# mLSTM cell and tanh-shrink MLP in fp32: scores on quarter tiles of the array that leave out the quarter under the diagonal

## The chip, the cores and the metric

The kernel runs on one core of one Trainium2 chip. The metric is the device time of one launch in microseconds (us); lower is better.

## What is computed

An mLSTM cell runs over 768 tokens for 4 batches and 8 heads of width 40, and its gated output feeds a small MLP with the activation h - tanh(h). Everything is fp32.

```
for t in range(S):                       # q, k, v: (4, 8, 768, 40)
    m_new = max(f[t] + m, i[t]);  fs = exp(f[t] + m - m_new);  is = exp(i[t] - m_new);  m = m_new
    C = fs * C + is * outer(v[t], k[t]);  n = fs * n + is * k[t]
    y[t] = sigmoid(o[t]) * (C @ q[t]) / max(abs(n . q[t]), 1)
x = y as (3072, 320);  h = x @ w_in (320, 2048);  out = (h - tanh(h)) @ w_out (2048, 320)
```

The kernel computes the recurrence in chunks: within a chunk of 128 tokens, token t needs the products q[t].k[s] for all s <= t (a square of scores of which only the part on and over the diagonal counts, when keys stand in rows and queries in columns), and for all earlier tokens the state at the chunk's start.

## The kernel before

**Units.** A unit is one chunk of 128 tokens of one batch: 6 chunks x 4 batches, 24 units, numbered so that unit n is chunk n // 4 of batch n % 4. Two units make a group of 256 tokens for the MLP; there are 12 groups. The MLP has 2048 hidden features, taken 256 at a time: 8 pairs for each group, two pairs to an item, four items to a group.

**Two stages.** The first 12 units (PLANNED, L1182) and the first 17 items are put in order by a planner with costs for each engine (Plan, L157, run at L1490). From item START (L1186) on, the order is written out by the loop at L1514. Each item of that loop has a dense list of matrix steps: the up products of this item (up, L1023, 16 instructions of 128 columns of weights and 256 tokens, then a remainder on 64 rows, since 320 = 128 + 128 + 64), then cell work, then the down products of the item before (down_seven, L911). The other 12 units each take a slot of two items: in the first, scores(n) follow the remainder (L1523); in the second, block_turned(n) does (L1525). merge (L1146) lays the steps of cell_slot (L853: scaling v, gates, stores) between. An engine carries out its instructions in the order in which this program issues them (Pinned, L96, and T, L116): nothing overtakes within an engine or a queue.

**A later unit's path.** load_unit (L342) issues kz, qz (features first, heads 0 to 3 in rows 0 to 39, heads 4 to 7 in rows 64 to 103), v, k and o on SP's queue, one slot ahead. scaled (L614) multiplies v by a number per token and head, out of ei. scores (L629) makes for each head a square of 128 keys by 128 queries, K = 40, in two banks of PSUM; the two row halves of the array work at once, each with the whole width of weights. mask (L639) multiplies by the matrix upto (ones where key <= query) on DVE and writes P. block_turned (L764) adds up the state's part (old state by qz) and the products of scaled v with P, with 64 x 64 tiles: the 128 keys are the two row halves r, two heads sit in the two column halves c. Row half r writes bank turned[r], so that the two banks have to be summed: turn_back (L807) copies one bank on ACT, adds on DVE, transposes in blocks of 32 on DVE and brings the result to token order by way of DRAM (h_rows, z_in) on SP's queue. gate_turned (L827) divides and gates, and turn_by_store (L735) brings y into xT, features first, again by way of DRAM (y_rows) on SP's queue. update_halves and keep_halves (L789, L800) make the next state out of k and the scaled v.

**Names.** upto (L381) is the 128 x 128 mask. ei (L423) holds the scales by token in rows and by chunk and head in columns; t["wide"] is the scaled v of a unit; HALF is 64, HH is 4, D is 40, D1 is 41 (the extra column gives the denominator). In up, quarters=True takes the remainder with 64 x 64 tiles (quarter, L1040) and False with 64 x 128 tiles (product, L1028); it is True in the items where block_turned follows. in_halves (L752) copies the states of the planned units to the layout of the later ones. PE has one line for all of its products (L129), and all other engines share L106.

Of the kernel before, what the change touches and what calls it, by code (L numbers as in the profile page):

```python
# [60 lines left out]
L = 128  # L61
# [18 lines left out]
def kernel(  # L80
# [258 lines left out]

    ld = {}  # L340

    def load_unit(n, names=("kz", "qz", "v", "k", "o", "q2"), queue=SP, behind=()):  # L342
        c, b = divmod(n, B)
        t = ld.setdefault(n, {})
        for name in names:
            if name in ("kz", "qz"):
                t[name] = load.tile([128, HH, L], FP, name=name, tag=name, bufs=3)
                for i in range(2):
                    src = kT if name == "kz" else qT
                    dma = queue.dma_start(out=t[name][i * HALF:i * HALF + D], in_=src[b, c, :, i * HH:(i + 1) * HH])  # L350
                    if behind:
                        tc.add_manual_dep(dma.ins, behind[-1].ins.name, SYNC, reason="order of transfers")
            elif name == "k":
                if n + B < NU:
                    t["k"] = load.tile([L, WIDE, D], FP, name="k", tag="k", bufs=3)
                    queue.dma_start(out=t["k"].rearrange("p h d -> p (h d)"),
                                    in_=bass.AP(k.tensor, k[b, c].offset, [[H * D, L], [1, WIDE * D]]))
            elif name != "q2":
                src, bufs = {"v": (v, 3), "o": (o_gate, 4)}[name]
                t[name] = load.tile([L, H, D], FP, name=name, tag=name, bufs=bufs)  # L360
                queue.dma_start(out=t[name], in_=src[b, c])
            elif c:
                t["q2"] = load.tile([TOP, len(TRIOS), L], FP, name="q2", tag="q2", bufs=3)
                for i in range(TRIO):
                    queue.dma_start(out=t["q2"][i * D:(i + 1) * D, 0:len(range(i, H, TRIO))], in_=qT[b, c, :, slice(i, H, TRIO)])
# [59 lines left out]


    eN = const.tile([TOP, NU, HH], FP, name="eN")

    begun = []

# [183 lines left out]
    def scaled(n, i, name, bufs, by_heads=False):  # L614
# [2 lines left out]
        flat = att.tile([L, H * D1 + HALF - D1], FP, name=name, tag=name, bufs=bufs)  # L617
        to = flat[:, 0:H * D1].rearrange("p (h d) -> p h d", d=D1)
        t["wide"] = flat
        scale = ei[:, i, t["c"], t["hs"]]  # L620
        t["column"] = lambda: A.copy(out=to[:, :, D], in_=scale)
        if by_heads:
            for h in range(H):
# [5 lines left out]
    def scores(n):  # L629
# [5 lines left out]
        def product(j, i):  # L635
            rows = slice(i * HALF, i * HALF + D)
            T.matmul(ps[i][:, j, :], t["kz"][rows, j, :], t["qz"][rows, j, :], start=True, stop=True)
# [12 lines left out]

        masks = [(lambda i=i: copy(i), lambda i=i: select(i)) if n in BY_POOL and not t.get("decays") else lambda i=i: mask(i) for i in range(2)]
        return [lambda j=j, i=i: product(j, i) for j in range(HH) for i in range(2)], masks

    def halves(*parts):

        for first in (0, 1):
            for steps in parts:
                for step in steps[first]:
                    step()
# [104 lines left out]
    def block_turned(n):  # L764
# [12 lines left out]
                    T.matmul(t["turned"][i][c * HALF:(c + 1) * HALF, i * 2 + g, :], old[rows, j * D1:j * D1 + HALF], t["qz"][rows, j, :],  # L777
                             start=(g == 0), stop=False, skip_group_check=True)
        for i in range(2):
            for g in range(2):  # L780
                for c in range(2):
                    for r in range(2):
                        rows, j = slice(r * HALF, (r + 1) * HALF), 2 * g + c
                        at = (i * HH + j) * D1
                        T.matmul(t["turned"][r][c * HALF:(c + 1) * HALF, i * 2 + g, :], t["wide"][rows, at:at + HALF], t["P"][rows, i, j, :],
                                 start=False, stop=True, skip_group_check=True)
        update_halves(n)

    def update_halves(n):  # L789
# [17 lines left out]
    def turn_back(n):  # L807
# [3 lines left out]
        both = att.tile([128, 2, HH * L // BLOCK, BLOCK], FP, name="zt", tag="P", bufs=4)  # L811
        zt, added = both[:, 0], both[:, 1].rearrange("p b i -> p (b i)")
        flat = zt.rearrange("p b i -> p (b i)")
        A.copy(out=added, in_=t["turned"][1].rearrange("p g t -> p (g t)"))
        V.tensor_tensor(out=added, in0=t["turned"][0].rearrange("p g t -> p (g t)"), in1=added, op=OP.add)
        V.transpose(flat, added)
        rows = dram.tile([2, 2, HH, L, BLOCK], FP, name="h_rows", tag=f"h_rows{n % 4}")
        for a in range(128 // BLOCK):
            half, low = divmod(a, 2)
# [33 lines left out]
    def cell_slot(s, o):  # L853
# [2 lines left out]
        steps, pause = [], [(0.0, lambda: None)]  # L856
        if s is not None:
            if s + 1 < NU and s + 1 not in ld:
                load_unit(s + 1, ("kz", "qz", "v", "k", "o"))
            begin(s)  # L860
        if o is None:
            return [(0.0, lambda: prepare(s))]
# [644 lines left out]
    for p in range(SPLIT):  # L1507
        spread_over([(0.0, lambda p=p: [step() for _, step in sums_of_weights(p)])], START + p / 2, START + 0.5 + p / 2)
    banks[:] = [name for name in ("b0", "b1") if name != third["tag"]]
    load_unit(PLANNED, ("kz", "qz", "v", "k", "o"))  # L1510
    for b in range(B):
        in_halves(b)
    news = []
    for x in range(START, len(items) + LAG):  # L1514
# [4 lines left out]
                new.append(slot[0])  # L1519
        if x < len(items):  # L1520
            some = tuple(run[:2] for run in items[x])
            dense, rest = up(some, shrink(x), bool(scored))
            dense.append((0.6 + 0.9 * len(new[:1]), lambda: halves(rest, *(scores(n) for n in new[:1]))))  # L1523
            for n in scored:
                dense.append((1.9, lambda n=n: [block_turned(n), Clock.later("turned", 1.2, lambda: [turn_back(n), n + B < NU and keep_halves(n)])]))  # L1525
        dense += [(0.9, lambda n=n: halves(scores(n))) for n in new[1 if x < len(items) else 0:]]
        some = tuple(run[:2] for run in items[x - LAG])
        if in_seven(*some[0]):
            dense += down_seven(some)
# [207 lines left out]
```

## Time and profile before

| | |
|---|---|
| runs, median of 3 | 520.84 us (517.76 to 527.25) |
| profiled execution | 518.27 us |
| its span, first to last instruction | 516.6 us |
| granted clock of the matrix engine | 0.999 |
| matrix products | 3993 instructions |
| DVE, ACT, POOL busy | 375.5, 206.1, 37.8 us |

PE is the matrix engine (matmuls), PEld its loads of weights, DVE the vector engine, ACT the scalar engine, POOL the GpSimd engine, SP the engine that only issues transfers (SPq: its queue). In the profile, a product such as ps<-qz,kz writes the tile ps out of kz and qz; a form such as 40*128 40x128 says that 40 rows and 128 columns of the array are used and 40 partitions x 128 elements move through. Each fp32 product shows as two instructions on PE. A piece of the timeline gives start, length, what ran and how many; [...]pieces overlap, and costs are read from start to start.

### The profile page before, as it was taken

How to read it: one execution, taken by the hardware profiler on the slowest of the kernel's cores; microseconds unless marked ns; L12 is line 12 of the kernel's file. 1: busy time of each engine (PE TensorE's matmuls, PEld its weight loads, DVE VectorE, ACT ScalarE, POOL GpSimd, SP SyncE). 2: the span in 40 equal slices, each digit the busy share in tenths (PEclk: the TensorE clock that was granted, in tenths of full speed). 3: DMA queues.
4: the chain of work that ended last, by engine and by line, in shares of the span. 5: the costliest groups of instructions: out<-in, count | busy, mean ns of one | idle time of the engine just before them, and what ended most of it. 6: DMA issues, size and time to landing. Idle time of an engine off the chain costs nothing.

```text
span 516.6 us, 10519 instructions
## 1 busy us (share of the span) xinstructions
PE 507.4 (98%) x3993; PEld 440.1 (85%) x3993; DVE 375.5 (73%) x828; ACT 206.1 (40%) x523; POOL 37.8 (7%) x75
## 2 busy tenths in 40 slices
PE   8999999999999999999999999999999999999995
PEld 5778878888898888898898899899889899898985
DVE  5999879998856658787768668668668668663734
ACT  4575697666444242242332242232233232232321
POOL 5423234120000000000000000000000000000000
PEclk9999999999999999999999999999999999999999
DMA  7987646340003000033533533533433432310001
GB/s 234 287 253 231 193 141 195 120 113 26 2 4 93 5 27 25 3 81 75 141 70 84 139 73 92 122 81 85 103 81 85 108 81 37 83 30 1 27 0 32
DMA packets 100385, 47.32 MB, mean 92 GB/s; under 512 B 75048, under 2 KB 94056, under 8 KB 100328
## 3 DMA queue, kind: packets, MB, share of 16 engines
q1 hardware_dynamic: 94096, 31.84, 25.7%
q0 software_dynamic: 3040, 10.82, 6.8%
q10 hardware_dynamic: 3192, 3.93, 2.2%
q8 instruction: 33, 0.54, 0.5%
q14 instruction: 24, 0.20, 0.1%
HBM read 36.91 MB, written 9.44 MB: 90 GB/s over the span
## 4 chain that ended last, share of the span: by engine, by line
PE 94%; DMA 2%; ACT 1%; POOL 1%; DVE 0%; issue 0%; SPq 0%; DVEq 0%
PE ph_up L129 42%; PE pS L129 31%; PE po L129 7%; PE ph L129 4%; PE ps L129 4%; PE pT L129 3%; PE pc L129 2%; DMA w<-in_moe_w_in 2%; PE px L133 1%; DMA w_out<-in_i_gate 0%; POOL w L106 0%; ACT vs L106 0%; PE awake L129 0%; ACT L106 0%; DVE w_in L106 0%
## 5 line engine op out<-in xcount | busy, mean ns | idle before, releaser
L129 PE MATMUL ph_up<-xT,w_in 128*128 128x256 f32 (+2 forms) x1248 | 227.5, 387 | 0.0
L129 PEld LDWEIGHTS ph_up<-xT,w_in 128*128 128x128 f32 (+2 forms) x1248 | 173.6, 180 | 36.3 <-issue 15.3
L106 ACT ACTIVATE z<-ph_up 128x512 f32<-128x512 f32 (+1 forms) x98 | 56.8, 583 | 245.9 <-PE ph_up L129 123.7
L106 DVE SCALAR_TENSOR_TENSOR gt<-ph_up,z 128x512 f32<-128x512 f32 (+1 forms) x98 | 63.5, 675 | 67.2 <-ACT z L106 66.9
L129 PE MATMUL pS<-wT,s 128*128 128x160 f32 x480 | 72.0, 299 | 0.0
L129 PEld LDWEIGHTS pS<-wT,s 128*128 128x128 f32 x480 | 67.4, 190 | 0.0
L106 ACT ACTIVATE q<-z,tiny 128x512 f32<-128x512 f32 (+1 forms) x98 | 66.3, 711 | 1.0
L106 DVE SCALAR_TENSOR_TENSOR gt<-q,gt 128x512 f32<-128x512 f32 (+1 forms) x98 | 63.2, 675 | 0.0
L129 PE MATMUL pS<-w_out,gt 128*128 128x160 f32 x320 | 54.3, 312 | 0.0
L106 DVE TENSOR_TENSOR P<-ps,upto 128x512 f32<-128x512 f32 x36 | 23.2, 685 | 41.4 <-PE ps L129 41.4
L129 PEld LDWEIGHTS pS<-w_out,gt 128*128 128x128 f32 x320 | 44.6, 189 | 7.5 <-issue 4.3
L129 PE MATMUL po<-w_out,gt 128*128 128x320 f32 x128 | 38.1, 441 | 0.0
L129 PEld LDWEIGHTS po<-w_out,gt 128*128 128x128 f32 x128 | 23.1, 190 | 8.5 <-issue 0.3
L106 DVE TENSOR_TENSOR s<-gt 128x256 f32<-128x256 f32 x80 | 30.2, 417 | 0.0
L129 PE MATMUL pS<-w_out,s 128*128 128x160 f32 x160 | 28.3, 299 | 0.0
L129 PE MATMUL pS<-wT,gt 128*128 128x160 f32 x160 | 28.3, 299 | 0.0
L129 PEld LDWEIGHTS ps<-qz,kz 40*128 40x128 f32 x384 | 25.1, 188 | 1.7 <-DVE inv L106 0.4
L129 PE MATMUL ps<-qz,kz 40*128 40x128 f32 x384 | 25.9, 274 | 0.0
L129 PEld LDWEIGHTS ph<-vs,P 128*128 128x128 f32 x192 | 23.9, 192 | 1.5 <-POOL P L106 1.1
L129 PE MATMUL ph<-vs,P 128*128 128x41 f32 x192 | 24.4, 273 | 0.6 <-POOL P L106 0.6
L129 PEld LDWEIGHTS pS<-w_out,s 128*128 128x128 f32 x160 | 23.9, 190 | 0.0
L129 PEld LDWEIGHTS pS<-wT,gt 128*128 128x128 f32 x160 | 23.9, 190 | 0.0
(107 smaller groups left out, 488.7 us busy)
## 6 DMA issues: line engine op xcount, KB each, us to landing
w<-in_moe_w_out POOLq DMA_DIRECT2D x8, 640.0 KB, 6.0
w<-in_moe_w_in POOLq DMA_DIRECT2D x16, 256.0 KB, 4.4
kz<-in_kT SPq DMA_DIRECT2D x48, 80.0 KB
o<-in_o_gate SPq DMA_DIRECT2D x24, 160.0 KB
k<-in_k SPq DMA_DIRECT2D x20, 180.0 KB
qz<-in_qT SPq DMA_DIRECT2D x44, 80.0 KB
v<-in_v SPq DMA_DIRECT2D x22, 160.0 KB
out<-ob ACTq DMA_DIRECT2D x11, 320.0 KB
```

What stands on the lines that cost most here:

```text
L106: i = method(*args, **kwargs)
L129: return cls.keep(nc.tensor.matmul(*args, **kwargs))
L133: return cls.keep(nc.tensor.transpose(*args, **kwargs))
```

## The change

For the 12 units of the second stage the chunk's square of scores is made in quarters of 64 x 64 and the one that the mask makes all zero (late keys, early queries) is left out, both in the scores and in the products of P with the scaled v.

Each head then needs a product of early keys with all queries (128 columns) and one of late keys with late queries (64 columns). To keep four 64 x 64 tiles at work, half of the heads (2 to 5) have their two halves of keys exchanged: their early keys stand in rows 64 to 127 of P. So the same heads have the token halves of k, v and the scales exchanged too: load_crossed loads k and v in three transfers each instead of one, and cross, once ahead of the stage, makes a copy of the scales with eight small transfers and the mask in quarters (over) on GpSimd. P then has three blocks of 64 queries instead of four quarters, so mask works on 384 elements per row instead of 512. In block_turned an early half of the queries gets its products from one row half only, and turn_back sums only where two banks hold a share. The remainder of up takes 64 x 64 tiles in items with new scores as well. The planner's stage, the MLP and the costs in the dense list stay as they are.

```diff
--- before.py
+++ after.py
@@ -339,11 +339,26 @@
 
     ld = {}
 
-    def load_unit(n, names=("kz", "qz", "v", "k", "o", "q2"), queue=SP, behind=()):
+    def load_crossed(to, src):
+        ends = [x.rearrange("t (n two) d -> t n two d", two=2)[:, ::HH - 1].rearrange("t n two d -> t n (two d)") for x in (to, src)]
+        SP.dma_start(out=ends[0], in_=ends[1])
+        for r in range(2):
+            SP.dma_start(out=to[r * HALF:(r + 1) * HALF, 2:6], in_=src[(1 - r) * HALF:(2 - r) * HALF, 2:6])
+    def load_unit(n, names=("kz", "qz", "v", "k", "o", "q2"), queue=SP, behind=(), crossed=False):
         c, b = divmod(n, B)
         t = ld.setdefault(n, {})
+        t["crossed"] = crossed
         for name in names:
-            if name in ("kz", "qz"):
+            if crossed and (name == "v" or name == "k" and n + B < NU):
+                whole = load.tile([L, H if name == "v" else WIDE, D], FP, name=name, tag=name, bufs=3)
+                t[name] = whole
+                if name == "k":
+                    G.memset(whole[:, H:], 0.0)
+                load_crossed(whole[:, 0:H], (v if name == "v" else k)[b, c])
+            elif name in ("kz", "qz"):
                 t[name] = load.tile([128, HH, L], FP, name=name, tag=name, bufs=3)
                 for i in range(2):
                     src = kT if name == "kz" else qT
@@ -426,6 +441,24 @@
 
     eN = const.tile([TOP, NU, HH], FP, name="eN")
 
+    crossed = const.tile([L, NT - NT // 2, BH], FP, name="crossed")
+    over = const.tile([L, 3, HALF], FP, name="over")
+    def cross():
+        to, src = (x.rearrange("t c (b h) -> t c b h", h=H) for x in (crossed, ei[:, 0, NT // 2:]))
+        for r in range(2):
+            rows, others = slice(r * HALF, (r + 1) * HALF), slice((1 - r) * HALF, (2 - r) * HALF)
+            for heads in (slice(0, 2), slice(6, 8)):
+                SP.dma_start(out=to[rows, :, :, heads].rearrange("t c b h -> t (c b) h"), in_=src[rows, :, :, heads].rearrange("t c b h -> t (c b) h"))
+            for heads in (slice(2, 4), slice(4, 6)):
+                SP.dma_start(out=to[rows, :, :, heads].rearrange("t c b h -> t (c b) h"), in_=src[others, :, :, heads].rearrange("t c b h -> t (c b) h"))
+        G.tensor_copy(out=over[:, 1], in_=upto[:, HALF:])
+        G.memset(over[:, 2], 1.0)
+        for r in range(2):
+            rows = slice(r * HALF, (r + 1) * HALF)
+            for k in range(0, 3 if r == 0 else 1, 2):
+                G.tensor_copy(out=over[rows, k], in_=upto[rows, r * HALF:(r + 1) * HALF])
     begun = []
 
     def gate_rows(c0, c1):
@@ -617,7 +650,7 @@
         flat = att.tile([L, H * D1 + HALF - D1], FP, name=name, tag=name, bufs=bufs)
         to = flat[:, 0:H * D1].rearrange("p (h d) -> p h d", d=D1)
         t["wide"] = flat
-        scale = ei[:, i, t["c"], t["hs"]]
+        scale = crossed[:, t["c"] - NT // 2, t["hs"]] if t["crossed"] else ei[:, i, t["c"], t["hs"]]
         t["column"] = lambda: A.copy(out=to[:, :, D], in_=scale)
         if by_heads:
             for h in range(H):
@@ -650,6 +683,30 @@
 
         masks = [(lambda i=i: copy(i), lambda i=i: select(i)) if n in BY_POOL and not t.get("decays") else lambda i=i: mask(i) for i in range(2)]
         return [lambda j=j, i=i: product(j, i) for j in range(HH) for i in range(2)], masks
+    def crossed_scores(n):
+        t = un[n]
+        ps = [ps_a.tile([L, 3, 2, HALF], FP, name="ps", tag=f"a{i}") for i in range(2)]
+        def product(i, c, kind, half):
+            rows, j, side = slice(i * HALF, i * HALF + D), 2 * (i ^ kind) + c, half ^ kind
+            where, late = slice(side * HALF, (side + 1) * HALF), slice(half * HALF, L)
+            to = ps[i][where, 1 + kind, c] if half else ps[i][where, 0:2 + kind:1 + kind, c]
+            q = t["qz"][rows, j, late]
+            T.matmul(to, t["kz"][rows, j, half * HALF:(half + 1) * HALF], q if half else q.rearrange("d (two t) -> d two t", two=2),
+                     start=True, stop=True, skip_group_check=True)
+        def mask(i):
+            V.tensor_tensor(out=over_diagonal(t["P"], i), in0=ps[i], in1=over.unsqueeze(2).to_broadcast([L, 3, 2, HALF]), op=OP.mult)
+        return [lambda i=i, c=c, kind=kind, half=half: product(i, c, kind, half)
+                for c in range(2) for kind, half in ((0, 0), (1, 0), (0, 1), (1, 1)) for i in range(2)], [lambda i=i: mask(i) for i in range(2)]
+    def over_diagonal(P, i):
+        return P[:, i].rearrange("p j t -> p (j t)")[:, 0:3 * L].rearrange("p (s c t) -> p s c t", s=3, c=2)
 
     def halves(*parts):
 
@@ -777,13 +834,14 @@
                     T.matmul(t["turned"][i][c * HALF:(c + 1) * HALF, i * 2 + g, :], old[rows, j * D1:j * D1 + HALF], t["qz"][rows, j, :],
                              start=(g == 0), stop=False, skip_group_check=True)
         for i in range(2):
-            for g in range(2):
+            P = over_diagonal(t["P"], i)
+            for kind, half in ((0, 0), (1, 0), (0, 1), (1, 1)):
                 for c in range(2):
-                    for r in range(2):
-                        rows, j = slice(r * HALF, (r + 1) * HALF), 2 * g + c
-                        at = (i * HH + j) * D1
-                        T.matmul(t["turned"][r][c * HALF:(c + 1) * HALF, i * 2 + g, :], t["wide"][rows, at:at + HALF], t["P"][rows, i, j, :],
-                                 start=False, stop=True, skip_group_check=True)
+                    g, r = i ^ kind, half ^ kind
+                    rows, at = slice(r * HALF, (r + 1) * HALF), (i * HH + 2 * g + c) * D1
+                    to = t["turned"][r][c * HALF:(c + 1) * HALF, i * 2 + g, half * HALF:]
+                    T.matmul(to if half else to.rearrange("d (two t) -> d two t", two=2), t["wide"][rows, at:at + HALF],
+                             P[rows, 1 + kind, c] if half else P[rows, 0:2 + kind:1 + kind, c], start=False, stop=True, skip_group_check=True)
         update_halves(n)
 
     def update_halves(n):
@@ -811,9 +869,12 @@
         both = att.tile([128, 2, HH * L // BLOCK, BLOCK], FP, name="zt", tag="P", bufs=4)
         zt, added = both[:, 0], both[:, 1].rearrange("p b i -> p (b i)")
         flat = zt.rearrange("p b i -> p (b i)")
-        A.copy(out=added, in_=t["turned"][1].rearrange("p g t -> p (g t)"))
-        V.tensor_tensor(out=added, in0=t["turned"][0].rearrange("p g t -> p (g t)"), in1=added, op=OP.add)
-        V.transpose(flat, added)
+        banks_of = [x.rearrange("p g t -> p (g t)") for x in t["turned"]]
+        A.copy(out=added[:, HALF:], in_=banks_of[1][:, HALF:])
+        V.transpose(flat[:, 0:HALF], banks_of[0][:, 0:HALF])
+        sums = [x.rearrange("p (i t) -> p i t", i=2)[:, :, HALF:] for x in (added, banks_of[0])]
+        V.tensor_tensor(out=sums[0], in0=sums[1], in1=sums[0], op=OP.add)
+        V.transpose(flat[:, HALF:], added[:, HALF:])
         rows = dram.tile([2, 2, HH, L, BLOCK], FP, name="h_rows", tag=f"h_rows{n % 4}")
         for a in range(128 // BLOCK):
             half, low = divmod(a, 2)
@@ -856,7 +917,7 @@
         steps, pause = [], [(0.0, lambda: None)]
         if s is not None:
             if s + 1 < NU and s + 1 not in ld:
-                load_unit(s + 1, ("kz", "qz", "v", "k", "o"))
+                load_unit(s + 1, ("kz", "qz", "v", "k", "o"), crossed=True)
             begin(s)
         if o is None:
             return [(0.0, lambda: prepare(s))]
@@ -1507,7 +1568,8 @@
     for p in range(SPLIT):
         spread_over([(0.0, lambda p=p: [step() for _, step in sums_of_weights(p)])], START + p / 2, START + 0.5 + p / 2)
     banks[:] = [name for name in ("b0", "b1") if name != third["tag"]]
-    load_unit(PLANNED, ("kz", "qz", "v", "k", "o"))
+    cross()
+    load_unit(PLANNED, ("kz", "qz", "v", "k", "o"), crossed=True)
     for b in range(B):
         in_halves(b)
     news = []
@@ -1519,11 +1581,11 @@
                 new.append(slot[0])
         if x < len(items):
             some = tuple(run[:2] for run in items[x])
-            dense, rest = up(some, shrink(x), bool(scored))
-            dense.append((0.6 + 0.9 * len(new[:1]), lambda: halves(rest, *(scores(n) for n in new[:1]))))
+            dense, rest = up(some, shrink(x), bool(scored or new[:1]))
+            dense.append((0.6 + 0.9 * len(new[:1]), lambda: halves(rest, *(crossed_scores(n) for n in new[:1]))))
             for n in scored:
                 dense.append((1.9, lambda n=n: [block_turned(n), Clock.later("turned", 1.2, lambda: [turn_back(n), n + B < NU and keep_halves(n)])]))
-        dense += [(0.9, lambda n=n: halves(scores(n))) for n in new[1 if x < len(items) else 0:]]
+        dense += [(0.9, lambda n=n: halves(crossed_scores(n))) for n in new[1 if x < len(items) else 0:]]
         some = tuple(run[:2] for run in items[x - LAG])
         if in_seven(*some[0]):
             dense += down_seven(some)
```

## The prediction, made before the changed kernel ran

> **What bounds the kernel now.** I read the page first, then the chain, then PE's timeline over one pair of items, then SP's waits. The first two lines are the page's busy times and its chain by engine.
>
> ```profile
> PE 507.4 (98%) x3993; PEld 440.1 (85%) x3993; DVE 375.5 (73%) x828; ACT 206.1 (40%) x523; POOL 37.8 (7%) x75
> ...
> PE 94%; DMA 2%; ACT 1%; POOL 1%; DVE 0%; issue 0%; SPq 0%; DVEq 0%
> ```
>
> The matrix engine is the bound: it is 98% of the span, and the chain that ended last is PE for 94% of it. The 2% of DMA is a load of weights in the first 20 us. From about 203 us to the last products PE has no idle at all, so what an item takes is the sum of what PE issues in it, and only a shorter list on PE shortens it. Next is PE's timeline around unit 12 (start, length, form, count; a form 64*64 means tiles of 64 rows by 64 columns of the array).
>
> ```profile
> 205.78 2.09 PE L129 MATMUL ph_up<-xT,w_in 128*128 128x256 f32 x12
> 207.70 1.06 PE L129 MATMUL ps<-qz,kz 40*128 40x128 f32 x16
> 208.69 1.35 PE L129 MATMUL pS<-w_out,gt 128*128 128x160 f32 x8
> ...
> 217.06 0.62 PE L129 MATMUL pT<-qz,state 40*64 40x128 f32 x16
> 217.50 1.05 PE L129 MATMUL pT<-P,vs 64*64 64x128 f32 x32
> 218.48 0.67 PE L129 MATMUL pc<-vs,k 128*64 128x41 f32 x16
> 219.08 1.35 PE L129 MATMUL pS<-w_out,gt 128*128 128x160 f32 x8
> ```
>
> A piece costs the time from its start to the start of the next. The scores (ps) cost 208.69 - 207.70 = 0.99 us, the products with values (pT<-P,vs) 218.48 - 217.50 = 0.98 us. Both appear 12 times (units 12 to 23). So all that the change can touch on PE is 12 x 1.97 = 23.6 us, 4.6% of the span, and a quarter of it is 5.9 us. That is the frame: no more than about 1% unless something breaks.
>
> **What a round costs.** Each fp32 product is two PE instructions. The start times of single instructions in the trace show how they run. In the pT piece four instructions, one for each 64*64 tile, start 6 to 7 ns apart, and the next four follow 108.5 ns after: a round of 128 columns. The scores run in rounds of two tiles (64 rows, all 128 columns of the array) with some 106 ns between rounds; 8 rounds. At the end of a piece, where the tile form changes, the last round takes about 0.10 to 0.11 us more (208 instead of 106 ns in ps, 219 instead of 108.5 in pT).
>
> A 64*64 round with 64 moving columns isn't in the trace, so I bound it. [...]Weights have to be loaded too: ph<-vs,P, of the first twelve units, has 41 columns and weights 128 wide, and its rounds are 111 ns apart; pc<-vs,k has the same 41 columns and weights 64 wide, and its rounds are 58 ns apart. So a load goes by its width, and 64 wide costs 58. Low end 53, nearest row 58. A rule speaks for a higher end: the Trainium skill, page "TensorE: Matmul & The Clock Gate", section "Wait — 56ns, not 53.3ns?", says that start to start never falls below about 25 ns, however few columns there are. Four tiles would then need 100 ns a round, and halving the columns would bring next to nothing. The trace has starts 6 to 7 ns apart when the tiles differ, so I read the rule as one for matmuls one behind the other in the same tile, and take **58 ns**. What the trace can't exclude is that such bursts come out of a filled queue and a long stretch is supplied more slowly. The longest stretch of small tiles now, from 216.14 to 219.08, is 160 PE instructions (loads and matmuls) in 2.94 us, 18.4 ns each, with no gap; the changed one would be 160 in 2.75 us, 17.2 ns each, only 6% denser.
>
> **The change, part by part.**
>
> Scores: 8 products of two-tile rounds become 16 products on 64*64 tiles: for each of two c, four tiles with 128 columns and four with 64, two instructions each. That is 4 x 108.5 + 4 x 58 = 666 ns, plus 0.11 for the end. In each second group of four the order of the tiles is swapped, and as starts go in order, a swap can hold the next round up by the 13 ns between first and third start: three swaps, 0 to 0.04 us. Between 0.78 and 0.82: I take **0.80**, against 0.99: -0.19 us.
>
> Products with values: 16 products as now, but half of them with 64 columns; the same rounds: 0.80 against 0.98: **-0.18 us**. The state's part (217.06) and pc stay.
>
> The up products' remainder in items with new scores goes from two-tile to four-tile form. Both forms are in the trace: in the items with a pT the four-tile form costs 0.914 us to the next piece (216.14 to 217.06), in those with ps the other costs 0.968: **-0.05 us**.
>
> Sum per unit 0.19 + 0.18 + 0.05 = 0.42 to 0.43; times 12, **-5.1 us**. Ends: with 100 ns rounds each piece is 0.94 to 0.98 and the sum is -1 to -2 us; if the swapped order let only two of the four tiles overlap, a round of 64 is 116 ns, each piece about 1.0, and only the remainder's 0.6 us is left, so about nothing; without swaps and with a shorter end, -6 to -7 us.
>
> Work beside PE, costed at nothing because PE covers it: the masks shrink from 128x512 (685 ns on DVE) to 128x384, 0.55 us by the 417 ns of a 128x256 row; turn_back's sum shrinks by 0.13 us and its transpose, now in two, grows by about as much; ACT's copy loses 0.05. DVE is 73% busy, so none of it shows. If DVE were the bound, this would bring some 3 us.
>
> SP's queue carries the new transfers. These are SP's waits, then its issues, start and length, and at 282.39 a line of PE (three windows of the timeline):
>
> ```profile
> SPq L106 <- DVE yt L106: 71.5, 12, 8.4
> ```
>
> ```profile
> 102.73 0.73 SPq L106 DMA_DIRECT2D kz<-in_kT  x2
> 103.50 0.71 SPq L106 DMA_DIRECT2D qz<-in_qT  x2
> 104.31 0.35 SPq L106 DMA_DIRECT2D v<-in_v  x1
> 114.60 0.35 SPq L106 DMA_DIRECT2D k<-in_k  x1
> ```
>
> ```profile
> 231.41 0.35 SPq L106 DMA_DIRECT2D v<-in_v  x1
> 231.87 0.37 SPq L106 DMA_DIRECT2D k<-in_k  x1
> ```
>
> ```profile
> 263.17 1.25 SPq L106 DMA_DIRECT2D xT<-y_rows  x2
> ```
>
> ```profile
> 282.39 0.81 PE L129 MATMUL ph_up<-xT,w_in 128*128 128x256 f32 x3
> ```
>
> The eight copies of cross() stand ahead of unit 12's kz, at 102.7. Each has 64 x 12 runs of 8 bytes; the nearest row, the SBUF to SBUF copies of the states, takes 0.71 us an issue, and h_rows, with 512 runs, 0.5. Say 0.7 to 1.0, so 6 to 8 us: SP is through by 111, while it waits until 114.60 for k's buffer anyway. Behind it stand unit 12's loads and the copies of in_halves; unit 12's scores come at 207.7. Even at 5 us each (40 us) the last states would be in place near 180. Cost 0. GpSimd's copies for the mask and its memsets stand in a queue that is empty from 115 on.
>
> In each later slot v and k take three issues each instead of one: 4 more, 0.35 to 0.5 us each, 1.4 to 2.0 us (2 issues in the last four units, which load no k). Behind them in SP's queue are y_rows, the reshaping by stores that feeds xT. SP now waits 71.5/12 = 6.0 us a slot for yt with nothing else to do: that covers it. Without that cover xT would be late; it is issued until 264.4 and first read at 282.39, so 16 us stand behind it (landing included) before PE waits. GpSimd's memset of k's last column waits for a buffer that SP's load waits for in the same way.
>
> **The time.** The profiled execution took 518.27 us, its span is 516.6, and 1.7 lie around it. Span 516.6 - 5.1 = 511.5, time 513.2. The median of the runs shown is 520.84, 2.6 above that execution, while the lowest is 517.76; carried over to the median the forecast is 515.7. The next median may fall at either place; I put it between, **514.5 us**.
>
> **The rivals.**
> Small rounds cost 100 ns or more (a limit of supply, or the swap breaks the overlap). For it: the rule, and that no 64-column round of four tiles is in the trace. Against: the stretch of 160 instructions without a gap. Time: 518.3 - 0.6 to 2 = 516 to 518 by the profiled execution, up to 520 by the median. Chance 0.22.
> More than the sum, with rounds at 53 and shorter ends: -6 to -7, so 511 to 512 (514 by the median). Chance 0.08.
> Slower, by SP's queue: if the four added issues each wait for an earlier transfer to land, they may cost 3 us instead of 0.4. It decides from 1.5 us each, where they eat the 6.0 us; at 3 us SP falls 6 us behind in each of 8 slots, 48 us, of which 16 are covered; 32 us reach PE: 518.3 - 5.1 + 32 = 545. For it: h_rows and y_rows do wait for landings. Against: three loads in a row (229.8 to 233) pass at 0.35 each. Chance 0.05.
> The forecast itself, -4 to -6: 0.65.
>
> **How the numbers follow.** The range takes the median's own place (3 us up or down), -7 at its low end and no gain at its high end: 510.5 to 521. A difference of 2%, about what a measurement of this kernel can tell from no change, is 10.4 us: under 510.4 the forecast case needs the largest gain and a low median (0.07); over 531.3 only the SP case (0.04 to 0.05); the rest, 0.88, is within.
>
> **What would show it.** Right: ps in form 40*64, 32 instructions, from its start to pS in 0.80 us; pT to pc in 0.80; the remainder 0.914 in every such item; a pair of items 19.4 us instead of 19.8; SP's wait for yt near 4 us a slot. The forecast fails if the 64-column rounds are not near 58 ns, or if PE shows idle before ph_up (xT late) or before pT (masks or vs late).

## The result, and the profile after

| | before | changed | changed over before, 95% interval |
|---|---|---|---|
| median | 519.17 us | 512.39 us | 0.9878 [0.9856, 0.9900] |
| lowest | 517.76 us | 511.12 us | |
| second measurement, median | 519.21 us | 511.62 us | 0.9872 [0.9850, 0.9895] |
| second measurement, lowest | 517.46 us | 510.61 us | |

The changed kernel is 1.2 to 1.3% faster, some 6.6 us. In the first profiled execution of the changed kernel (520.63 us) the matrix engine's pieces took nearly twice as long until 27.4 us (a first piece of 16 instructions for scores 2.08 us instead of 1.21), before the change has any part in it, so the lines below are from the profile of the second measurement (an execution of 510.61 us, span 508.9, granted clock 1.000).

The page of the changed kernel, busy times and chain by engine:

```profile
PE 501.7 (99%) x4281; PEld 434.4 (85%) x4281; DVE 371.8 (73%) x840; ACT 205.6 (40%) x523; POOL 39.6 (8%) x88
...
PE 96%; DVE 1%; ACT 1%; POOL 1%; DMA 0%; issue 0%; SPq 0%; DVEq 0%
```

PE has 288 more matmul instructions, 24 in each of 12 units (16 for the scores, 8 for the remainder, whose tiles are half as wide), and yet is busy 5.7 us less. It is still the bound, and the chain is still PE. The timeline of PE around unit 12, start, length, form, count:

```profile
206.92 0.85 PE L129 MATMUL ps<-qz,kz 40*64 40x128 f32 x32
207.70 1.35 PE L129 MATMUL pS<-w_out,gt 128*128 128x160 f32 x8
...
216.06 0.62 PE L129 MATMUL pT<-qz,state 40*64 40x128 f32 x16
216.50 0.85 PE L129 MATMUL pT<-P,vs 64*64 64x128 f32 x32
217.28 0.67 PE L129 MATMUL pc<-vs,k 128*64 128x41 f32 x16
```

From start to start the scores take 207.70 - 206.92 = 0.78 us, and the products with values 217.28 - 216.50 = 0.78 us. No bracket with idle time stands behind a line: PE waits for nothing here, and the two pieces have simply become shorter. The next unit's scores start at 226.25, so two items take 19.33 us instead of 227.50 - 207.70 = 19.80.

SP's waits for yt, and its issues in two windows (start, length, what, how many):

```profile
SPq L106 <- DVE yt L106: 36.4, 11, 8.3
```

```profile
102.00 6.92 SPq L106 DMA_DIRECT2D crossed<-ei  x8
...
113.87 1.55 SPq L106 DMA_DIRECT2D k<-in_k  x3
```

```profile
271.53 1.57 SPq L106 DMA_DIRECT2D v<-in_v  x3
273.21 2.35 SPq L106 DMA_DIRECT2D k<-in_k  x3
```

The eight copies of cross() hold the queue for 6.92 us and are over before k's buffer comes free, as before the change. In the slots SP's spare time has gone from 71.5 to 36.4 us, 2.9 us a slot on average. The average hides where it went. Taken wait by wait, the six slots that load both v and k had 5.8 us each to spare and have 1.2 left (one has none); the four that load only v went from 5.7 to 3.9, and the last two, which load nothing, are unchanged. So four added issues take 4.6 us out of the cover of a slot.

**Where the 7.65 us between the two clean profiles (spans 516.56 and 508.90 us) come from.** I cut the span at the start of item START and at the small product that writes the tile count, some 3 us ahead of PE's last product, and summed PE's pieces from start to start. In the profile of before that product is

```profile
507.45 0.19 PE L129 MATMUL count<-ones,most 128*1 128x1 f32 x2
```

| stretch | before | changed | difference |
|---|---|---|---|
| planner's stage, to item START | 203.2 | 202.5 | -0.7, and other profiles that leave this stage as it is lie between 202.4 and 203.5 |
| scores, 12 pieces, mean of one | 0.989 | 0.779 | -2.52 |
| products with values, 12 pieces | 0.986 | 0.780 | -2.47 |
| up's remainder ahead of them, 12 pieces | 0.968 | 0.914 | -0.64 |
| end of the run with its closing barrier, from count | 9.1 | 7.8 | -1.3 |

PE's pieces bring 5.63 us. The last row belongs to none of the steps of the prediction and is looked into below (i).

### The profile page after: what moved, and what is told of

The parts are those of the page before. It is cut to its first block, busy times and chain, and to the rows that moved or that the text cites. A ratio compares the mean times of both kernels' runs of the same rounds, so it can differ in the third digit from the quotient of the medians.

```text
span 518.8 us, 11220 instructions
## 1 busy us (share of the span) xinstructions
PE 512.1 (99%) x4281; PEld 441.9 (85%) x4281; DVE 371.7 (72%) x840; ACT 205.6 (40%) x523; POOL 40.3 (8%) x88
## 3 DMA queue, kind: packets, MB, share of 16 engines
q1 hardware_dynamic: 106128, 31.72, 27.3%
## 4 chain that ended last, share of the span: by engine, by line
PE 98%; ACT 1%; DVE 0%; issue 0%
PE ph_up L129 41%; PE pS L129 31%; PE po L129 7%; PE ph L129 5%; PE ps L129 4%; PE awake L129 3%; PE pT L129 3%; PE pc L129 2%; PE px L133 1%; ACT vs L106 0%; PE gate L129 0%; ACT L106 0%; PE gate L133 0%; DVE ob L106 0%; ACT part L106 0%; ACT o L106 0%
## 5 line engine op out<-in xcount | busy, mean ns | idle before, releaser
L129 PEld LDWEIGHTS ph_up<-xT,w_in 128*128 128x128 f32 (+2 forms) x1344 | 171.5, 173 | 37.3 <-issue 15.3
L106 DVE TENSOR_TENSOR P<-ps,over 128x384 f32<-128x384 f32 x24 | 12.3, 553 | 36.4 <-PE ps L129 36.4
L129 PEld LDWEIGHTS ph<-vs,P 128*128 128x128 f32 x192 | 27.4, 215 | 1.0 <-issue 0.6
L129 PEld LDWEIGHTS ps<-qz,kz 40*64 40x64 f32 (+1 forms) x576 | 25.1, 163 | 3.2 <-DVE vs L106 0.8
L129 PE MATMUL ph<-vs,P 128*128 128x41 f32 x192 | 27.5, 294 | 0.0
L129 PE MATMUL ps<-qz,kz 40*128 40x128 f32 (+2 forms) x576 | 26.1, 267 | 0.0
```

The source lines that it names most:

```text
L106: i = method(*args, **kwargs)
L129: return cls.keep(nc.tensor.matmul(*args, **kwargs))
```

## The experiments

Each starts from the changed kernel unless it says otherwise. Prices of pieces are from start to start, means of 12; "lowest" is the fastest run, which I compare with the fastest of the kernel before on the same chip. "The loop" is PE's time from item START to count in a run's trace: 304.3 us before, 298.6 in both profiles of the changed kernel. It scatters far less than whole runs do, so small differences are read from it.

**Half of the saving undone (a, b, c).** In a the scores take all 128 queries again, in the same 64 x 64 tiles and the same order; the masked quarter is computed and not used.

```diff
-        ps = [ps_a.tile([L, 3, 2, HALF], FP, name="ps", tag=f"a{i}") for i in range(2)]
+        ps = [ps_a.tile([L, 4, 2, HALF], FP, name="ps", tag=f"a{i}") for i in range(2)]
...
-            to = ps[i][where, 1 + kind, c] if half else ps[i][where, 0:2 + kind:1 + kind, c]
-            q = t["qz"][rows, j, late]
+            to = ps[i][where, 0:3 + kind:2 + kind, c] if half else ps[i][where, 1:3 + kind:1 + kind, c]
+            q = t["qz"][rows, j, :]
...
```

> The changed kernel with only the scores made whole again: the products of late keys take all 128 queries, and the extra 64 columns go to a block of the bank that nothing reads. My account (the change pays by the columns that PE no longer moves): 64-column rounds become 128-column ones, each about 54 ns longer, 4 in a unit, so the scores' piece goes from 0.78 back to about 0.99 us and the time is 2.5 us over the changed kernel, 3.8 under the one before (ratio near 0.993). If the gain came from the shorter masks or sums on the vector engine, which this kernel keeps, it would stay at the changed kernel's ratio, 0.988.

Measured: 513.88 us, ratio 0.9894 [0.9876, 0.9913], lowest 513.41. The timeline of its PE:

```profile
207.53 1.05 PE L129 MATMUL ps<-qz,kz 40*64 40x128 f32 x32
208.51 0.68 PE L129 MATMUL pS<-w_out,gt 128*128 128x160 f32 x3
```

The same 32 instructions take 0.98 us again: it is the number of columns that makes the piece shorter, not the tiles. The ratio alone would not say so, since its interval overlaps that of the changed kernel; the loop does: 301.1 us, 2.5 more than in the changed kernel, as expected.

In b the products with values take all 128 queries, with zeros in the quarter that is put back (P gets a fourth block and a memset on GpSimd), and the scores stay cut.

```diff
+            G.memset(over_diagonal(t["P"], i)[:, 0], 0.0)
...
-                             P[rows, 1 + kind, c] if half else P[rows, 0:2 + kind:1 + kind, c], start=False, stop=True, skip_group_check=True)
+                             P[rows, 0:3 + kind:2 + kind, c] if half else P[rows, 1:3 + kind:1 + kind, c], start=False, stop=True, skip_group_check=True)
```

> The changed kernel with only the products with values made whole again: the late keys' rows of P get a block of zeros for the early queries (one more memset on GpSimd for each half), and their products take 128 columns. My account: the piece goes from 0.78 to about 0.99 us, the time is 2.5 us over the changed kernel, ratio near 0.993. If the swap of the tiles' order or anything else than the columns set the piece, it would stay near 0.78.

Measured: 515.94 us, 0.9926 [0.9901, 0.9950], lowest 513.61. By its trace the piece is back at 0.985 us, the scores stay at 0.779, and the loop takes 301.1 us. As in a, half of the saving is gone.

c does both: no product is cut, but the exchanged loads, cross() and four-tile scores are all there.

> Both products made whole again, in the exchanged layout with all of its transfers, copies and 64 x 64 tiles. My account: all that is beside PE costs nothing, so only the gain of the remainder (0.05 us in 12 items, 0.6 us) is left: ratio 0.998 to 1.000 against the kernel before. If the exchanged loads, the eight copies of the scales or GpSimd's part had a hidden price that the shorter products pay for, this kernel would be slower than the one before by that price, over 1.002.

Measured: 516.71 us, 0.9947 [0.9926, 0.9967], lowest 515.70. I expected a gain of 0.6 us, and it is 2 us by the lowest runs. In its trace PE's pieces are 0.985, 0.985 and 0.914: -0.7 us, all from the remainder, and the loop takes 303.6 us. For about 1 us of the rest the closing barrier (i) is the likely cause, but c's own profile does not show it: there SP comes to the barrier later than before (8.0 us after count instead of 7.3), and from count to the end it takes 8.9 us. What c was made for is clear: exchanging token halves adds nothing to PE's loop. Lowest runs against those of before: a -4.3, b -4.1, c -2.0, changed -6.6 us. So each saving taken alone brings some 2.2 us over c, and the two add up.

**The remainder's form (d, e, h).** d leaves the remainder of up in two-tile form where scores follow:

```diff
-            dense, rest = up(some, shrink(x), bool(scored or new[:1]))
+            dense, rest = up(some, shrink(x), bool(scored))
```

> The changed kernel with the remainder of up as it was in the items with new scores (64 x 128 tiles, followed by scores on 64 x 64). My account: 0.97 us as before plus a change of form between remainder and scores, 0.05 to 0.10, so 1.02 to 1.07 us instead of 0.914, 12 times: 1.2 to 1.9 us over the changed kernel, ratio near 0.991. If changes of form are free, 0.6 us over it.

Measured: 515.09 us, 0.9910 [0.9893, 0.9926], lowest 513.26. e makes the opposite edit in the kernel before, whose scores keep their two-tile form:

```diff
-            dense, rest = up(some, shrink(x), bool(scored))
+            dense, rest = up(some, shrink(x), bool(scored or new[:1]))
```

> The kernel before with only the remainder of up on 64 x 64 tiles in the items with new scores, whose two-tile scores stay. My account: the remainder alone saves 0.05 us and a change of form ahead of the scores costs about 0.10, so each of 12 items loses 0.05 us: 0 to 0.6 us slower than the kernel before, ratio 1.000 to 1.001. If the four-tile form is cheaper by itself, 0.6 us faster (0.999).

Measured: 520.97 us, 1.0040 [1.0020, 1.0059]. That is a loss of 1.9 us by the lowest runs, more than expected. Its timeline:

```profile
207.79 1.16 PE L129 MATMUL ps<-qz,kz 40*128 40x128 f32 x16
208.88 0.54 PE L129 MATMUL pS<-w_out,gt 128*128 128x160 f32 x2
```

Now the two-tile scores take 1.09 us where they took 0.99. Put side by side:

| | remainder | scores | both |
|---|---|---|---|
| before: two tiles, then two | 0.968 | 0.989 | 1.957 |
| e: four, then two | 1.024 | 1.092 | 2.116 |
| d: two, then four | 1.064 | 0.828 | 1.892 |
| changed: four, then four | 0.914 | 0.779 | 1.693 |

Compare rows in which a piece has the same form: where its neighbour's form differs, the remainder takes 0.10 us (1.064 against 0.968) or 0.11 (1.024 against 0.914) more, and the scores 0.05 (0.828 against 0.779) or 0.10 (1.092 against 0.989). So a change of form between neighbouring pieces costs 0.15 to 0.21 us. The Trainium skill, page "TensorEngine Tiling (Array Packing)", section "Key Properties", says that changing the tiling mode drains the engine; it gives no price. These rows give one, and they agree with it, though none of them shows the draining itself. In d the two pieces together lose 1.892 - 1.693 = 0.20 us a unit, 2.4 us in all (the loop takes 301.0 us), and its lowest run is 2.1 us above the changed kernel's: a little more than expected, because the scores behind the other form lose 0.05 us too.

h takes the quarter form in every item and in the planner's stage too.

```diff
-            dense, rest = up(some, shrink(x), bool(scored or new[:1]))
+            dense, rest = up(some, shrink(x), True)
...
```

> The changed kernel with the remainder of up on 64 x 64 tiles in every item, the planned ones too, where a change of form to the whole array follows. By my account the four-tile form needs less weight loading in the open, 0.05 us an item in some 25 items more: 1.2 us under the changed kernel, ratio near 0.9855. If the saving is only in having the same form as the scores, no difference from the changed kernel.

Measured: 513.26 us, 0.9881 [0.9845, 0.9917], lowest 511.30. I expected 1.2 us less than the changed kernel. By the trace the loop is 0.3 us shorter than in the changed kernel (eight items have a remainder of 1.024 instead of 1.064 us), while the planner's stage in this profile ends at 204.1 us; nothing shows in the times. It is no better version.

**What a round costs (f).** Ahead of the state's part, block_turned gets 8 rounds of products (16 of instructions) on four tiles for each of 128, 64, 32 and 16 columns; their results are overwritten by what follows.

```diff
+        for size in (128, 64, 32, 16):
+            for _ in range(8):
+                for c in range(2):
+                    for i in range(2):
+                        rows = slice(i * HALF, i * HALF + D)
+                        T.matmul(t["turned"][i][c * HALF:(c + 1) * HALF, 0, 0:size], old[rows, c * D1:c * D1 + HALF], t["qz"][rows, c, 0:size],
+                                 start=True, stop=True, skip_group_check=True)
```

> The changed kernel with 16 rounds each of 128, 64, 32 and 16 moving columns on four 64 x 64 tiles added ahead of the state's part in 12 units; their results are overwritten. It measures the price of a round by its columns, in a stretch of 128 products (256 matmuls) without large ones. My account: 128 columns 108 ns, 64 columns 55, and no less with 32 and 16, since the 64-wide weights still have to be loaded; about 4.4 us more in each unit, some 53 us in all. A limit of supply would show as 64-column rounds that grow to 80 to 100 ns once the queue is empty. If only columns count, 32 and 16 would fall to 27 to 30 ns.

One execution: 606.65 us, span 604.9. Starts of rounds are 108 to 110 ns apart with 128 columns and 58 to 59 ns with 64, with 32 and with 16. So a round has a floor of 58 ns whatever its columns, and 64 columns are already at it. That the loading of weights 64 wide sets it fits pc<-vs,k (58 ns) and ph<-vs,P (111 ns with weights 128 wide), but no run changes the width of the weights alone. There is no floor of 100 ns. In the changed kernel itself the short rounds are 55 and 59 ns apart, and the swap of the tiles' order leaves no trace.

But the loop is 85 us longer, and the rounds make only 12 x 4.54 = 54.5 of it. The waits of PE, one stretch of its timeline (idle time in brackets) and the page's row for transfers of instructions:

```profile
PE pT L129 <- issue: 11.2, 14, 1.3
```

```profile
228.74 1.98 PE L129 MATMUL pT<-qz,state 40*64 40x128 f32 x114
231.49 1.99 PE L129 MATMUL pT<-qz,state 40*64 40x32 f32 x105 [0.77 <-issue]
```

```profile
q8 instruction: 60, 0.98, 0.7%
```

PE stops in 16 places for 0.5 to 1.5 us, each time a multiple of 256 of its instructions (loads and matmuls) after the last stop, some 16 us in all. The q8 row has 60 transfers where the changed kernel has 36, and the 24 more are the 6144 added instructions by 256. In the loop these transfers come no closer than 3.4 us, which is some 13.5 ns for an instruction (estimated from 3.4 to 3.5 us over 256): these short rounds, which take their instructions faster, run dry. The rest goes to the clock: the granted clock was at half in seven windows of 3.4 to 6.8 us, 27.3 us together, half of which is lost; that makes 54.5 + 16 + 13.7 = 84 us. Each of these windows begins within 1.4 us of the end of a stop, though no stop was longer than 1.5 us; why some stops are followed by one and others are not, no run here shows.

**SP's queue (g).** The loads of load_crossed are cut into four times, and into two times as many transfers.

```diff
-        SP.dma_start(out=ends[0], in_=ends[1])
+        step = HALF // 4
+        for x in range(0, L, 2 * step):
+            SP.dma_start(out=ends[0][x:x + 2 * step], in_=ends[1][x:x + 2 * step])
         for r in range(2):
-            SP.dma_start(out=to[r * HALF:(r + 1) * HALF, 2:6], in_=src[(1 - r) * HALF:(2 - r) * HALF, 2:6])
+            for x in range(0, HALF, step):
+                SP.dma_start(out=to[r * HALF + x:r * HALF + x + step, 2:6], in_=src[(1 - r) * HALF + x:(1 - r) * HALF + x + step, 2:6])
```

> The changed kernel with each of the three transfers of an exchanged load cut into four, by rows: 24 instead of 6 issues a slot for v and k. By my account SP has about 3 us a slot left in the changed kernel; 18 more issues at 0.4 us are 7.2, so SP falls some 4 us behind in each of 7 or 8 slots, about 30 us, of which 16 are covered: PE waits for xT near the end of the stage, 10 to 20 us over the changed kernel. If the loads are hidden in any case, as the rival has it that SP never reaches the path, the time stays at the changed kernel's.

Measured: 545.68 us, 1.0518 [1.0488, 1.0549], lowest 545.10: 34 us over the changed kernel, more than expected. PE's timeline, SP's issues and DVE's timeline around one wait of PE:

```profile
290.70 0.71 PE L129 MATMUL pS<-w_out,s 128*128 128x160 f32 x4
297.29 2.93 PE L129 MATMUL ph_up<-xT,w_in 128*128 128x256 f32 x6 [5.89 <-DVE gt L106]
```

```profile
285.59 1.50 SPq L106 DMA_DIRECT2D xT<-y_rows  x2
...
290.96 1.90 SPq L106 DMA_DIRECT2D z_in<-h_rows  x4
```

```profile
295.04 0.17 DVE L106 SCALAR_TENSOR_TENSOR den<-z_in,inv 128x8 f32<-128x8 f32 x1 [11.93 <-DMA z_in<-h_rows]
...
296.55 1.28 DVE L106 SCALAR_TENSOR_TENSOR gt<-ph_up,z 128x512 f32<-128x512 f32 x2
```

PE waits 5.89 us ahead of up, and what it waits for is not xT. The packets of that xT (384 of 512 bytes) had all moved by 288.6 us. PE resumes at 297.29, right after the first of the two gt (0.69 us from 296.55): gt reads ph_up, and PE needs that buffer for the next products. DVE was late with gt because den<-z_in stands ahead of it in DVE's order and waited 11.93 us for z_in, the other way through DRAM, whose loads SP issued only at 290.96. It is so in all six waits (24.0 us together): before each den<-z_in is held up on DVE for 5.7 to 12.0 us, and PE resumes some 50 ns after the gt behind it. So a late SP queue reaches PE by way of h_rows, z_in and DVE, not by way of xT.

In the slots that load v and k, SP now takes 24.4 to 26.7 us from one xT to the next, where PE needs 19.3. In each of the four longer waits (4.2 to 6.0 us) the granted clock falls to half for 6.8 us, most of it behind the wait, and the six up products of the line above take 2.93 us where six take 1.56 in g_loads_x2; in the two shorter ones (1.6 and 2.0 us) it stays full. The Trainium skill, page "TensorE: Matmul & The Clock Gate", section "What's actually happening", gives a window of 3413 ns of idle or activity for the switch; the windows seen here are one or two of these. A wait costs more than its length: 24.0 us of waits and half of the 20.5 us at half clock behind them make 34 of the 36.7 us by which the loop is longer than in the changed kernel. I had left the clock out of the expectation.

> The changed kernel with each transfer of an exchanged load cut in two: 12 instead of 6 issues a slot for v and k. Six more issues at 0.42 us are 2.5 us of the 2.9 us that SP still waits for yt in a slot. My account: the cover just holds or is overrun by less than the 16 us behind xT, so the time stays within 1 us of the changed kernel, ratio 0.987 to 0.990. If the price of a transfer were in the moving and not in the issue, PE would already wait for xT in this kernel.

Measured: 515.46 us, 0.9937 [0.9915, 0.9959], lowest 512.54 against 510.61 of the changed kernel on the same chip: 1.9 us more by the lowest runs and 3.4 by the ratios, where at most 1 was expected. The loop takes 300.4 us, 1.7 more. SP's issues in one slot, and DVE ahead of PE's only wait in the loop:

```profile
231.04 3.28 SPq L106 DMA_DIRECT2D v<-in_v  x6
234.42 3.28 SPq L106 DMA_DIRECT2D k<-in_k  x6
```

```profile
356.40 0.17 DVE L106 SCALAR_TENSOR_TENSOR den<-z_in,inv 128x8 f32<-128x8 f32 x1 [7.05 <-DMA z_in<-h_rows]
```

From the first of v to the end of k's issues v and k take 6.7 us, in the same slot of the changed kernel 3.4. Six more issues cost 3.3 us, and the changed kernel has 1.2 us to spare in such a slot. So SP falls further behind from slot to slot, DVE's wait for z_in grows with them to 7.05 us, and there PE waits 1.1 us. In the changed kernel DVE waits for z_in twice, 1.0 us in all: the cover is nearly used up in these six slots.

**The closing barrier (i).** At the end of a run all engines answer a barrier. In the trace of before, DVE answers 8.76 us after count, the others at 7.6; in the changed kernel, a, b, c, d and h DVE answers together with the others. Those kernels have 30 to 33 more DVE instructions in all, e none, and in e DVE is late as well (8.64 us). So i adds 32 memsets of a small tile on DVE to the kernel before, and nothing else:

```diff
+        for _ in range(2 if x < START + 16 else 0):
+            V.memset(probe, 0.0)
```

> The kernel before with 32 tiny memsets added on DVE (two at the head of each of 16 items), nothing else. The traces leave about 1 us of the gain outside of PE's pieces: in the kernel before DVE answers the closing barrier at 8.8 us after the count, all other engines at 7.6, and in the changed kernel, which has 32 DVE instructions more, DVE answers with the others. If that is where DVE's instructions happen to end (a fetch at the very end), the stall at the barrier goes with these 32 memsets: the time from the count to the end falls from 9.1 to about 8.1 us, ratio near 0.998. If it belongs to what the changed kernel does, it stays at 9.1 and the ratio at 1.000.

Measured: 517.43 us, 0.9981 [0.9960, 1.0001], lowest 516.71 against 517.46. In the trace DVE is no longer late (7.41 us) and the kernel ends 8.07 us after count instead of 9.10; its loop takes 304.3 us, as before. The trace is plain, the timed interval just reaches 1. So about 1 us of the gain comes with the number of DVE's instructions, which the change raises by accident. Why DVE is late stays open. A late transfer of its instructions would fit, but the traces do not show one: the row q14 has a transfer near 7 us after count in before (7.03) and in i (7.02) alike.

**The change once more (k)**, unaltered, beside g_loads_x2 and i:

> The changed kernel as it is, once more, beside the two others on one chip and for a profile without the long cold start of its first one. Expected ratio 0.986 to 0.989; from item START to the end 306.7 us again, and the count to the end 8.1 us.

Measured: 511.62 us, 0.9872 [0.9850, 0.9895]; from item START to the end 306.4 us, from count to the end 7.8. The first measurement holds.

## Why the prediction was right, point by point

**The bound and the mechanism** were right. PE was the bound, its pieces became shorter, everything else stayed hidden. The sum was -5.1 us, and PE's pieces brought -5.63. Every piece came out as forecast to within 0.03 us.

**The time** was put at 514.5 us, between two places for the median, and is 512.39; against the profiled execution it was 513.2, and is 510.61. The pieces account for 0.5 of this, and the closing barrier, which the forecast did not have, for about 1; the rest is within the scatter of single runs. By its number alone, -6.6 us, the result lies in the rival "more than the sum" (-6 to -7, chance 0.08). Its reason, rounds at 53 ns and shorter ends, is not what happened: the short rounds take 55 to 59 ns.

**Scores**: -0.19 us forecast, -0.210 measured. **Values**: -0.18 forecast, -0.206 measured. In both the new piece was set at 0.80 and is 0.78. The 0.02 was the allowance for the swap of tiles, which leaves no trace; for values a further 0.006 is the single reading of 0.98 before, against a mean of 0.986. The value of 58 ns for a round of 64 columns, read off pc<-vs,k, was right in f (58 to 59) and in the kernel (55 and 59). One reading was off and changed nothing in the sum: the two-tile rounds of the scores before start 110 to 113 ns apart; the 106 read off, half of which is the low end of 53, is the pause from the second start of a round to the next round.

**The rule of 25 ns** that spoke against the change doesn't hold between different tiles: the starts of one round stay 6 to 7 ns apart with 64 columns too, and f's rounds of 16 columns come every 58 ns. Had it held, c and the changed kernel would have been nearly equal; they are 4.6 us apart by their lowest runs.

**The remainder**: -0.05 us forecast, -0.053 measured. The number was right for a reason that I had not put right: I took 0.914 as the price of the four-tile form as such. It is the price of that form ahead of the same form. On its own (e) the step loses 0.16 us a unit, and leaving it out of the change (d) loses 0.20. The two edits belong together.

**The supply of PE** was left open in the forecast at 17.2 ns an instruction. In f it runs out at about 13.5 ns, and the change, at 17.0 ns over the same stretch of 160 instructions, stays clear of it.

**The work beside PE.** The mask takes 553 ns for 0.55 forecast, and none of DVE's or ACT's work shows. cross() took 6.92 us for 6 to 8.

**SP's queue** is the part that was too kind, though it decided nothing. Four more issues a slot were put at 1.4 to 2.0 us. They occur in six slots, and take 4.6 us of the cover there; SP's wait for yt is 1.2 us in these slots and 3.0 on average, not near 4. The issues themselves were taken too cheap, at the 0.35 to 0.5 us of a single load: in the window shown v's three take 1.57 us and k's 2.35, together 3.2 more than two loads of 0.35. Why k's take longer there than v's no run here shows (in the slot at 231 us they take 1.69). The path was wrong as well: the 16 us behind xT are not what protects PE. The path that breaks first is z_in, through DVE, and in these runs PE begins to wait when DVE is held up there for about 5.7 us. That g_loads_x4 takes the 545 us of the rival "slower, by SP's queue" is luck: that sum had 32 us by way of xT and nothing for the clock, and the run has 24.0 us of waits by way of z_in and some 10 from the clock.

**What was not foreseen** is the closing barrier, about -1 us. Taken together, 5.6 + 1.0 = 6.6 us is what the lowest runs of the two kernels differ by (517.76 - 511.12). The same account fits the others within 0.6 us: a -4.2 for -4.3 measured, b -4.2 for -4.1, c -1.7 for -2.0, d -4.2 for -4.4, h -6.9 for -6.4, and e +1.9 for +1.9 with nothing from the barrier. **Open** stays how these split within the scatter of single runs: SP's own arrival at the barrier differs by up to 1.1 us from profile to profile (in c's it hides the gain), and the planner's stage, where it is the same, by 1.1 us.

## What to carry to other kernels

Where one engine is busy all the time, price an edit by that engine's pieces from start to start, and price the piece together with its neighbours: on the matrix engine pieces of the same tile form belong side by side. Cutting the columns of a round pays only down to a floor (here 58 ns, reached at 64 columns with weights 64 wide). Before crediting the cover of a queue, take its wait slot by slot and not as an average, count how many issues fit, and follow every path that hangs on the queue: here DVE, working in order, passed a late load on to work that did not need it. And look at the end of the run before the last microsecond is put down to the edit.

## What the runs showed of the hardware

- **Supply of instructions.** In f, PE stood still 0.5 to 1.5 us at multiples of 256 instructions, with transfers no closer than 3.4 us in the loop; in the changed kernel, at 17 ns an instruction over its densest stretch, it did not stop. The Trainium skill, page "Runtime: NRT & Kernel Launch", section "Instruction fetch mechanics", says that instructions come in blocks of 256, which agrees, and that fetching them is mostly hidden, which does not hold in f.
- **A change of tile form** costs 0.15 to 0.21 us over two neighbouring pieces (d, e); a change in the order of tiles within a form leaves no trace (in a, the rounds of the scores stay 108 to 109 ns apart across it).
- **A round on four 64 x 64 tiles** costs 108 to 110 ns with 128 columns and 58 to 59 with 64, 32 or 16 (f).
- **Waits of PE** of 4.2 to 6.0 us brought a granted clock of one half for 6.8 us, all four of them; two of 1.6 and 2.0 us did not (g_loads_x4). In f, half-clock windows of 3.4 to 6.8 us also came with stops of 0.9 to 1.5 us.
- **A late load on DVE's way** held up PE: den<-z_in stood on DVE for 5.7 to 12.0 us, the gt behind it freed PE's buffer late, and PE waited 1.6 to 6.0 us (g_loads_x4).
- **The end of a run**, from count on, took 1.0 us less with 32 more instructions on DVE (i); the cause is open.
